# Top-32 attention and expert layer: the mask and the exponential of a score row by two ScalarE passes

## The chip, the core and the metric

The kernel runs on one core of a Trainium2 chip. The time is the device time of one execution in microseconds, as a median over runs. TensorE (PE in the profile) multiplies matrices, VectorE (DVE) and ScalarE (ACT) work on rows of 128 partitions, GpSimd (POOL) takes simple passes over data outside PSUM, and SyncE (SP) issues the DMAs.

## What is computed

Two layers follow each other. The first is attention over 4 batches of 8 heads, 576 positions and 64 channels, in which each row of scores keeps only its 32 largest entries. The second is a layer of 8 experts, to which every token goes, weighted by a gate matrix P that is normalised by rows and columns eight times.

```python
scores = scale * np.matmul(q, k.transpose(0, 1, 3, 2))
kth = np.partition(scores, -top_k, axis=-1)[..., -top_k:-top_k + 1]
scores = np.where(scores >= kth, scores, -1000000000.0)
scores = scores - np.max(scores, axis=-1, keepdims=True)
attn = np.exp(scores)
attn = attn / (np.sum(attn, axis=-1, keepdims=True) + 1e-09)
attn_out = np.matmul(attn, v)
...
for e in range(E):
    h = np.maximum(x @ w1[e], 0.0)
    out += P[:, e:e + 1] * (h @ w2[e])
```

## The kernel before

**Attention.** A unit is a tile of 128 score rows by 576 columns. There are 144 of them: 64 pairs of two heads (`attend_phase`), and 16 single ones for the left-over rows (`rest_weights`). For each unit TensorE writes the scores into the one PSUM buffer `sp` (L118, L119), and ScalarE copies them into one of three buffers `s` (`copy_scores`, L125 and L127). `topk` then finds the 32nd largest entry on VectorE: four rounds of an instruction that gives the eight largest (L138), with the ones already found overwritten in a work tile `w` between the rounds (L145). After the first round GpSimd makes the negative maximum `nb` (L140), and ScalarE the exponential of the whole row into `Et` (L141). After the fourth round VectorE compares the scores with the 32nd and multiplies the exponential with the result (L147), which also gives the row sum into `st`. `normalise` adds a small number on GpSimd (L151), inverts on VectorE (L152) and scales on ScalarE (L154). TensorE transposes the weights (L235), they are split into a high and a low part, `ath` and `atl`, multiplied with the values, and summed into `xt` (L252).

**Experts.** The seven entries of `STAGES` say which blocks of 256 tokens attention makes in which order; the first three stages have 8 pairs of units each. The gate matmuls of a stage (L337) come at its end. When a block is ready it boards a seat (`board`) and is taken past the eight experts in turns (`visit`: L420 and L507, evictions at L469, L470 and L515). Weights are split on ScalarE and GpSimd (L77, L83). While the first stage still runs, `first_half` makes partial products of the first block at low priority (L450). The last four blocks go through `hidden_pair` and `last_outputs` (L618, L677), after all of attention, after the gate's normalisation and after `right_factors`.

**Order.** A scheduler puts the instructions of each engine in a fixed order when the program is built. Attention has high priority, evictions of expert products a higher one, and expert matmuls fill the rest. On the chip each engine runs its list in order, and waits at its head.

Of the kernel before, what the change touches and what calls it, by code (L numbers as in the profile page):

```python
# [7 lines left out]
F32 = mybir.dt.float32  # L8
F32R = mybir.dt.float32r
AF = mybir.ActivationFunctionType  # L10
OP = mybir.AluOpType
# [7 lines left out]
NFT = F // 128  # L19
TOPK = 32  # L20
LOWEST = -3.0e38

# [21 lines left out]
def kernel(  # L46
# [11 lines left out]
    nc = tc.nc  # L58
# [14 lines left out]
    ap_ = actx.enter_context(tc.tile_pool(name="ap", bufs=2, side="right"))  # L73
# [56 lines left out]
    def topk(units):  # L130
        n = len(units)
        ws = [ap_.tile([128, S], F32, name="w", bufs=2) for _ in units]
        m8 = [ap_.tile([128, 4, 8], F32, name="m8", bufs=6) for _ in units]
        nb = [ap_.tile([128, 1], F32, name="nb", bufs=6) for _ in units]
        for r in range(4):
            for u in range(n):
                s, Em, rsum = units[u]
                nc.vector.max(m8[u][:, r, :], ws[u] if r else s)  # L138
                if r == 0:
                    nc.gpsimd.tensor_scalar(nb[u], m8[u][:, 0, 0:1], -0.125, 1.0, op0=OP.mult, op1=OP.mult)  # L140
                    nc.scalar.activation(Em, s, AF.Exp, bias=nb[u], scale=0.125)  # L141
            for u in range(n):
                s, Em, rsum = units[u]
                if r < 3:
                    nc.vector.match_replace(ws[u], m8[u][:, r, :], ws[u] if r else s, LOWEST)  # L145
                else:
                    nc.vector.scalar_tensor_tensor(Em, s, m8[u][:, 3, 7:8], Em,  # L147
                                                   op0=OP.is_ge, op1=OP.mult, accum_out=rsum)

    def normalise(Et, st, n):  # L150
        nc.gpsimd.tensor_scalar(st[:, 0, 0:n], st[:, 0, 0:n], 1e-9, 1.0, op0=OP.add, op1=OP.mult)  # L151
# [61 lines left out]
    def attend_phase(hp, qs, qm, ks, xt, xm, off):  # L213
# [3 lines left out]
        for t in range(2):  # L217
            Et = ap_.tile([128, 2, S], F32, name="Et", bufs=2)
            st = ap_.tile([128, 2, 2], F32, name="st", bufs=3)
            units = []  # L220
            for i in range(2):
                o = i * 256 + t * 128
                qc = qs[:, o:o + 128]
                sp = scores([((a, 0, 288), [(qc, ks[i], slice(a * 288, a * 288 + 288))]) for a in range(2)])
                units.append((copy_scores(sp[:, :, 0:288]), Et[:, i, :], st[:, 0, i:i + 1]))
            topk(units)
            normalise(Et, st, 2)
            cs = slice(t * 128, (t + 1) * 128)
            Ef = Et.rearrange("p a b -> p (a b)")
            for g in range(3):  # L230
                ps = pst.tile([128, 4, 128], F32, name="pt")
                for r in range(3):
                    j = g * 3 + r
                    o = j * 128 if j < 4 else (j * 128 + 128 if j < 8 else 512)
                    nc.tensor.transpose(ps[:, r, :], Ef[:, o:o + 128], idt)  # L235
                put = evac_pool if g < off else evac
                put(ath[:, g * 3:g * 3 + 3, cs], atl[:, g * 3:g * 3 + 3, cs], ps[:, 0:3, :])
# [20 lines left out]
    def rest_weights(qm, ks, put):  # L258
        Et = ap_.tile([128, 2, S], F32, name="Et", bufs=2)
        st = ap_.tile([128, 2, 2], F32, name="st", bufs=3)  # L260
        qa, qb = qm[:, 0:128], qm[:, 128:256]
        sp = scores([
            ((0, 0, 256), [(qa, ks[0], slice(0, 256)), (qb, ks[1], slice(64, 320))]),
            ((0, 256, 512), [(qa, ks[0], slice(256, 512)), (qb, ks[1], slice(320, 576))]),
            ((1, 0, 64), [(qa, ks[0], slice(512, 576)), (qb, ks[1], slice(0, 64))]),
        ])
        topk([(copy_scores(sp.rearrange("p a b -> p (a b)")[:, 0:S]), Et[:, 0, :], st[:, 0, 0:1])])
        normalise(Et, st, 1)
        ps = pst.tile([128, 4, 128], F32, name="pt")
        for j in range(4):  # L270
            nc.tensor.transpose(ps[:, j, :], Et[:, 0, j * 128:(j + 1) * 128], idt)
        for i in range(2):
            put(slice(0, 128), slice(4 * i, 4 * i + 4), ps[:, :, i * 64:(i + 1) * 64])
        ps = pst.tile([128, 4, 128], F32, name="pt")
        nc.tensor.transpose(ps[0:64, 0, :], Et[:, 0, 512:576], idt)
        nc.tensor.transpose(ps[:, 1, :], Et[:, 0, 448:576], idt)
        for i, r in enumerate((va, vb)):
            put(r, 8, ps[r, i, r])
# [504 lines left out]
```

## Time and profile before

| What | Value |
|---|---|
| Median of 3 runs | 1977.47 us |
| Lowest and highest run | 1975.19 and 1978.46 us |
| Profiled execution: span from first to last instruction (the page gives no other time of it) | 1976.5 us |
| Mean granted TensorE clock, as a share of full speed | 0.979 |
| ScalarE busy | 1042.2 us (53%) |
| GpSimd busy | 1094.3 us (55%) |
| DMA traffic | 240.02 MB, 121 GB/s of HBM over the span |

Busy time of an engine is the time in which it had an instruction in work; the rest of the span it waited, at the head of its list, for another engine, a buffer or a DMA. Matmuls overlap, and their ends are modelled, so that TensorE's busy time shows where it had work and not how close to its peak it ran. Busy time of different engines overlaps and does not add up to the span.

### The profile page before, as it was taken

Reading aid. Unit: us, or ns where it says so; the run is one execution under the profiler, and the core shown is the slowest. Engines: PE = TensorE matmul, PEld = TensorE weight load, DVE = VectorE, ACT = ScalarE, POOL = GpSimd, SP = SyncE. Lnnn points to the kernel's source line nnn. Section 1 sums busy time; section 2 is a strip of 40 time slices with the busy share of each in tenths; the row PEclk is TensorE's granted clock in tenths of the full one; section 3 lists DMA queues with packets and bytes.
Section 4 is the critical chain, followed back from the end, with each engine's and each line's share of the span. In section 5 each row is a group of like instructions: output and inputs, shape, how many; then the busy total and the mean of one; then the engine's idle time right before and its main releaser. Section 6 shows DMA issues by size and latency. Waiting matters only on the chain.

```text
span 1976.5 us, 27330 instructions
## 1 busy us (share of the span) xinstructions
PE 1886.2 (95%) x9617; PEld 1591.8 (81%) x9617; DVE 1468.7 (74%) x2828; ACT 1042.2 (53%) x1705; POOL 1094.3 (55%) x978
## 2 busy tenths in 40 slices
PE   4798899899999999999999999999999999999998
PEld 3687788898888888888788888888888888888887
DVE  8999999999999999948999982225555555543333
ACT  5777767665666666655665654453333333333331
POOL 4558867546655544545544548984454544545440
PEclk8899999999999999999999998999999999999999
DMA  3477654434433423443423333543333333311111
GB/s 115 129 243 258 206 183 156 147 105 132 132 109 122 132 83 98 153 143 123 129 84 120 99 107 107 182 155 110 102 102 112 112 112 101 102 59 54 59 38 43
DMA packets 96073, 240.02 MB, mean 121 GB/s; under 512 B 10816, under 2 KB 12992, under 8 KB 95936
## 3 DMA queue, kind: packets, MB, share of 16 engines
q1 hardware_dynamic: 95936, 238.28, 37.6%
q8 instruction: 75, 1.23, 0.3%
q14 instruction: 62, 0.51, 0.1%
HBM read 203.64 MB, written 34.60 MB: 121 GB/s over the span
## 4 chain that ended last, share of the span: by engine, by line
PE 53%; DVE 36%; POOL 3%; DMA 3%; issue 3%; ACT 2%; SPq 0%; POOLq 0%; ACTq 0%; DVEq 0%
PE p L677 18%; DVE m L138 12%; DVE w L145 10%; PE p L618 9%; PE p L420 7%; PE p L507 7%; DVE Et L147 6%; PE pc L618 5%; DVE hl L470 3%; DVE atl L86 3%; PE pb L618 2%; POOL wl L83 2%; DMA wr<-in_w_dram 1%; PE p L450 1%; PE pt L235 1%
## 5 line engine op out<-in xcount | busy, mean ns | idle before, releaser
L83 POOL TENSOR_TENSOR wl<-wr,wh 128x1024 fp32r<-128x1024 f32 x280 | 681.4, 2445 | 423.8 <-ACT wh L77 408.0
L77 ACT ACTIVATE wh<-wr 128x1024 fp32r<-128x1024 f32 x280 | 294.5, 1059 | 276.8 <-PE p L618 183.5
L138 DVE MAX8 m<-w 128x8 f32<-128x576 f32 x432 | 317.0, 747 | 1.4
L420 PE MATMUL p<-xh,wh 128*128 128x256 f32 (+1 forms) x768 | 267.3, 348 | 9.2 <-DVE hl L470 9.2
L420 PE MATMUL p<-xh,wl 128*128 128x256 f32 (+1 forms) x768 | 263.9, 344 | 0.0
L420 PE MATMUL p<-xl,wh 128*128 128x256 f32 (+1 forms) x768 | 263.5, 343 | 0.0
L507 PE MATMUL p<-wh,hh 128*128 128x512 f32 x640 | 253.8, 400 | 7.0 <-ACT hh L469 7.0
L507 PE MATMUL p<-wl,hh 128*128 128x512 f32 x640 | 252.9, 398 | 0.0
L507 PE MATMUL p<-wh,hl 128*128 128x512 f32 x640 | 245.6, 396 | 1.9 <-DVE hl L470 1.9
L524 DVE SCALAR_TENSOR_TENSOR acc<-p,P,acc 128x512 f32<-128x512 f32 x120 | 89.5, 750 | 166.6 <-PE p L677 166.6
L145 DVE MATCH_REPLACE8 w<-m,w 128x576 f32<-128x576 f32 x288 | 212.8, 740 | 0.2
L677 PE MATMUL p<-wh,h2h 128*128 128x512 f32 x512 | 199.8, 391 | 1.3 <-ACT h2h L641 0.7
L677 PE MATMUL p<-wl,h2h 128*128 128x512 f32 x512 | 199.9, 390 | 0.0
L677 PE MATMUL p<-wh,h2l 128*128 128x512 f32 x512 | 196.7, 390 | 0.0
L147 DVE SCALAR_TENSOR_TENSOR Et<-s,m,Et 128x576 f32<-128x576 f32 x144 | 172.5, 1203 | 2.5 <-ACT Et L141 2.0
L420 PEld LDWEIGHTS p<-xh,wh 128*128 128x128 f32 x768 | 148.8, 194 | 29.9 <-DVE hl L470 13.9
L470 DVE SCALAR_TENSOR_TENSOR hl<-p,hh 128x512 fp32r<-128x512 f32 x160 | 108.1, 678 | 79.9 <-ACT hh L469 79.2
L420 PEld LDWEIGHTS p<-xl,wh 128*128 128x128 f32 x768 | 148.8, 194 | 15.0 <-DVE xl L86 0.3
L420 PEld LDWEIGHTS p<-xh,wl 128*128 128x128 f32 x768 | 148.7, 194 | 14.3
L507 PEld LDWEIGHTS p<-wh,hh 128*128 128x128 f32 x640 | 121.3, 190 | 29.3 <-ACT hh L469 8.4
L507 PEld LDWEIGHTS p<-wh,hl 128*128 128x128 f32 x640 | 120.7, 189 | 25.0 <-DVE hl L470 2.7
L507 PEld LDWEIGHTS p<-wl,hh 128*128 128x128 f32 x640 | 121.6, 190 | 22.7
(174 smaller groups left out, 4039.1 us busy)
## 6 DMA issues: line engine op xcount, KB each, us to landing
wr<-in_w_dram SPq DMA_DIRECT2D x240, 512.0 KB, 3.5
y<-y SPq DMA_DIRECT2D x160, 256.0 KB, 2.7
raw<-in_k_dram SPq DMA_DIRECT2D x56, 288.0 KB, 3.1
wr<-in_w_dram SPq DMA_DIRECT2D x48, 256.0 KB, 3.8
raw<-in_q_dram SPq DMA_DIRECT2D x32, 256.0 KB, 2.8
p<-y SPq DMA_DIRECT2D x32, 256.0 KB, 3.5
y<-p SPq DMA_DIRECT2D x32, 256.0 KB, 4.5
raw<-in_v_dram SPq DMA_DIRECT2D x28, 288.0 KB, 3.0
```

Of the source, the lines that this page charges most:

```text
L77: nc.scalar.activation(dst, src, AF.Copy)
L83: nc.gpsimd.tensor_tensor(dst, src, hi.bitcast(F32), op=OP.subtract)
L86: nc.vector.tensor_tensor(dst, src, hi.bitcast(F32), op=OP.subtract)
L138: nc.vector.max(m8[u][:, r, :], ws[u] if r else s)
L145: nc.vector.match_replace(ws[u], m8[u][:, r, :], ws[u] if r else s, LOWEST)
L147: nc.vector.scalar_tensor_tensor(Em, s, m8[u][:, 3, 7:8], Em, op0=OP.is_ge, op1=OP.mult, accum_out=rsum)
L420: nc.tensor.matmul(ps[:, fo, :], a[:, kk, fs], x[:, k0 + kk, cs], start=(i == 0), stop=(i == 3 * nk - 1))
L470: nc.vector.scalar_tensor_tensor(seat.hl[:, ft, cs], src, 0.0, seat.hh[:, ft, cs].bitcast(F32), op0=OP.max, op1=OP.subtract)
L507: nc.tensor.matmul(ps, a[:, ft, ts], m[:, ft % 2, :], start=(i == 0), stop=(i == 3 * NFT - 1))
L524: return nc.vector.scalar_tensor_tensor(ACC[t], y, g, ACC[t], op0=OP.mult, op1=OP.add)
L618: nc.tensor.matmul(ps, w[:, kk, :], x[:, kk, :], start=(fresh and i == 0), stop=(i == 5), skip_group_check=True)
L677: nc.tensor.matmul(ps, a[:, ft, ts], m[:, ft, :], start=(i == 0), stop=(i == 11))
```

## The change

The exponential no longer runs early. VectorE's compare-and-multiply goes. When the 32nd largest entry t of a row is known, ScalarE makes two passes over the unit. The first is a Prelu of t - s: entries at or above t give zero or a negative number that is multiplied by a slope of 2 to the power -100, entries below t stay positive and large. The second is an exponential that undoes the slope in its scale, so that kept entries give exp(0.125 (s - max)) and the others nothing, and it leaves the row sum. Its bias `eb` is a new small VectorE instruction for each pair (0.125 t + nb), and `nb` is now made once for a pair. Maxima, `nb` and `eb` now have one tile each for a pair.

```diff
--- before.py
+++ after.py
@@ -19,6 +19,10 @@
 NFT = F // 128
 TOPK = 32
 LOWEST = -3.0e38
+
+
+
+KEPT = 2.0 ** -100
 
 
 
@@ -130,22 +134,22 @@
     def topk(units):
         n = len(units)
         ws = [ap_.tile([128, S], F32, name="w", bufs=2) for _ in units]
-        m8 = [ap_.tile([128, 4, 8], F32, name="m8", bufs=6) for _ in units]
-        nb = [ap_.tile([128, 1], F32, name="nb", bufs=6) for _ in units]
+        m8 = ap_.tile([128, 2, 4, 8], F32, name="m8", bufs=3)
+        nb = ap_.tile([128, 2], F32, name="nb", bufs=3)
+        eb = ap_.tile([128, 2], F32, name="eb", bufs=3)
         for r in range(4):
             for u in range(n):
-                s, Em, rsum = units[u]
-                nc.vector.max(m8[u][:, r, :], ws[u] if r else s)
-                if r == 0:
-                    nc.gpsimd.tensor_scalar(nb[u], m8[u][:, 0, 0:1], -0.125, 1.0, op0=OP.mult, op1=OP.mult)
-                    nc.scalar.activation(Em, s, AF.Exp, bias=nb[u], scale=0.125)
-            for u in range(n):
-                s, Em, rsum = units[u]
-                if r < 3:
-                    nc.vector.match_replace(ws[u], m8[u][:, r, :], ws[u] if r else s, LOWEST)
-                else:
-                    nc.vector.scalar_tensor_tensor(Em, s, m8[u][:, 3, 7:8], Em,
-                                                   op0=OP.is_ge, op1=OP.mult, accum_out=rsum)
+                nc.vector.max(m8[:, u, r, :], ws[u] if r else units[u][0])
+            if r == 0:
+                nc.gpsimd.tensor_scalar(nb[:, 0:n], m8[:, 0:n, 0, 0], -0.125, 1.0, op0=OP.mult, op1=OP.mult)
+            if r < 3:
+                for u in range(n):
+                    nc.vector.match_replace(ws[u], m8[:, u, r, :], ws[u] if r else units[u][0], LOWEST)
+        nc.vector.scalar_tensor_tensor(eb[:, 0:n], m8[:, 0:n, 3, 7], 0.125, nb[:, 0:n],
+                                       op0=OP.mult, op1=OP.add)
+        for u, (s, Em, rsum) in enumerate(units):
+            nc.scalar.activation(Em, s, AF.Prelu, bias=m8[:, u, 3, 7:8], scale=-1.0, alpha=KEPT)
+            nc.scalar.activation(Em, Em, AF.Exp, bias=eb[:, u:u + 1], scale=-0.125 / KEPT, accum_out=rsum)
 
     def normalise(Et, st, n):
         nc.gpsimd.tensor_scalar(st[:, 0, 0:n], st[:, 0, 0:n], 1e-9, 1.0, op0=OP.add, op1=OP.mult)
```

Lines after `KEPT` stand four further down in the new file up to the change, so that L81 in it is L77 before, L131 is L127, L155 to L158 are L151 to L154; L142 and L147 are the old L138 and L145, and L148, L151 and L152 are new. The scheduler orders the whole program anew. The places that matter are on VectorE and ScalarE.

VectorE, first stage, before: the end of the first pair (maxima `m8_150` and `m8_151`, weights `Et_132`) and the beginning of the second (`m8_220`, `m8_221`).

```order
L138 MAX m8_150<-w_148 128x8
L138 MAX m8_151<-w_149 128x8
L147 SCALAR_TENSOR_TENSOR Et_132,st_133<-s_139,m8_150,Et_132 128x576
L145 MATCH_REPLACE w_218<-m8_220,s_209 128x576
L145 MATCH_REPLACE w_149<-m8_151,w_149 128x576
L138 MAX m8_220<-w_218 128x8
L138 MAX m8_221<-s_216 128x8
L138 MAX m8_151<-w_149 128x8
L145 MATCH_REPLACE w_218<-m8_220,w_218 128x576
L147 SCALAR_TENSOR_TENSOR Et_132,st_133<-s_146,m8_151,Et_132 128x576
L145 MATCH_REPLACE w_219<-m8_221,s_216 128x576
L138 MAX m8_220<-w_218 128x8
```

The same place in the changed program, where `m8_150` belongs to the first pair and `m8_219` to the second.

```order
L142 MAX m8_150<-w_148 128x8
L142 MAX m8_150<-w_149 128x8
L147 MATCH_REPLACE w_217<-m8_219,s_208 128x576
L147 MATCH_REPLACE w_149<-m8_150,w_149 128x576
L142 MAX m8_219<-w_217 128x8
L142 MAX m8_219<-s_215 128x8
L142 MAX m8_150<-w_149 128x8
L147 MATCH_REPLACE w_217<-m8_219,w_217 128x576
L148 SCALAR_TENSOR_TENSOR eb_152<-m8_150,nb_151 128x2
L147 MATCH_REPLACE w_218<-m8_219,s_215 128x576
L142 MAX m8_219<-w_217 128x8
L142 MAX m8_219<-w_218 128x8
```

The two masks are gone from between the maxima; one `eb` stands two instructions behind the pair's last maximum, and maxima of the second pair stand on both sides of it.

ScalarE, before, from the fourth score copy on: `s_216` is the second unit of the second pair, `s_335` the first of the third.

```order
L127 ACTIVATE s_216<-sp_211 128x576
L141 ACTIVATE Et_202<-s_216,nb_223 128x576
L127 ACTIVATE s_335<-sp_330 128x576
L154 ACTIVATE Et_132<-Et_132,st_133 128x576 x2
L162 ACTIVATE tl_182<-pt_178 128x384
L77 ACTIVATE ath_130<-tl_182 128x3x128
L141 ACTIVATE Et_328<-s_335,nb_348 128x576
L162 ACTIVATE tl_190<-pt_186 128x384
L77 ACTIVATE ath_130<-tl_190 128x3x128
L127 ACTIVATE s_342<-sp_337 128x576
```

And in the changed program, where `s_215` is the fourth copy and `s_333` the fifth.

```order
L151 ACTIVATE Et_132<-s_139,m8_150 128x576
L131 ACTIVATE s_215<-sp_210 128x576
L151 ACTIVATE Et_132<-s_146,m8_150 128x576
L152 ACTIVATE Et_132,st_133<-Et_132,eb_152 128x576 x2
L131 ACTIVATE s_333<-sp_328 128x576
L158 ACTIVATE Et_132<-Et_132,st_133 128x576 x2
L166 ACTIVATE tl_181<-pt_177 128x384
L151 ACTIVATE Et_201<-s_208,m8_219 128x576
L81 ACTIVATE ath_130<-tl_181 128x3x128
L131 ACTIVATE s_340<-sp_335 128x576
L166 ACTIVATE tl_189<-pt_185 128x384
```

Before, the exponentials stand behind the score copies of their own units and ahead of the mask. Now the Prelus and exponentials of the first pair (L151, L152) stand ahead of the fifth copy, with the fourth copy between the two Prelus, and the scaling (L158) follows close behind. The table load stands once in each program, at the start:

```order
L77 ACT_TABLE_LOAD
```

```order
L81 ACT_TABLE_LOAD
```

## Rows read from the trace of the kernel before

**Rows 1.** Page, busy us (share of span) by engine, and tenths by slice

```profile
PE 1886.2 (95%) x9617; PEld 1591.8 (81%) x9617; DVE 1468.7 (74%) x2828; ACT 1042.2 (53%) x1705; POOL 1094.3 (55%) x978
...
PE   4798899899999999999999999999999999999998
...
DVE  8999999999999999948999982225555555543333
```

**Rows 2.** Stretches: length; busy us of PE, PEld, DVE, ACT, POOL; clock, DMA

```profile
0.00:138.00 138.00, 94.87 (x450) 78.21 (x450) 131.44 (x280) 93.20 (x167) 74.27 (x117) 0.88 0.50 156
138.00:274.00 136.00, 120.25 (x691) 103.61 (x689) 134.57 (x259) 96.39 (x157) 105.45 (x95) 0.94 0.67 220
274.00:407.00 133.00, 124.88 (x818) 113.23 (x819) 131.16 (x263) 85.66 (x142) 83.89 (x88) 0.97 0.48 156
407.00:575.00 168.00, 163.72 (x923) 142.25 (x922) 165.08 (x341) 109.84 (x187) 95.29 (x97) 0.99 0.40 126
575.00:1214.00 639.00, 632.45 (x3345) 536.64 (x3344) 565.91 (x1176) 396.25 (x686) 328.24 (x320) 0.99 0.36 115
1214.00:1310.00 96.00, 89.69 (x533) 79.97 (x533) 26.59 (x81) 42.30 (x54) 90.59 (x52) 0.96 0.48 154
1310.00:1976.00 666.00, 660.38 (x2868) 537.95 (x2866) 313.92 (x432) 218.58 (x316) 316.59 (x213) 1.00 0.28 88
```

**Rows 3.** Groups by line to 1214 us: busy us, mean ns, then idle before

```profile
L147 DVE SCALAR_TENSOR_TENSOR Et<-s,m,Et 128x576 f32<-128x576 f32 x144 | 172.5, 1203 | 2.5 <-ACT Et L141 2.0
...
L138 DVE MAX8 m<-s 128x8 f32<-128x576 f32 x144 | 107.2, 744 | 11.4 <-ACT s L127 7.7 <-ACT s L125 3.5
L141 ACT ACTIVATE Et<-s,nb 128x576 f32<-128x576 f32 x144 | 106.6, 774 | 15.6 <-POOL nb L140 8.9 <-PE pt L235 6.6
...
L235 PE MATMUL pt<-idt,Et 128*128 128x128 f32 x576 | 97.1, 288 | 12.0 <-ACT Et L154 5.8 <-DVE xt L252 3.2 <-DVE atl L86 2.6
...
L127 ACT ACTIVATE s<-sp 128x576 f32<-128x576 f32 x128 | 83.0, 649 | 89.3 <-DVE Et L147 78.1 <-PE sp L119 7.8 <-PE p L420 2.6
L118 PE MATMUL sp<-kh,qs 128*128 128x288 f32 x256 | 83.0, 335 | 42.4 <-ACT s L127 37.4 <-ACT kh L77 5.0
...
L140 POOL TENSOR_SCALAR nb<-m 128x1 f32<-128x1 f32 x144 | 33.2, 231 | 167.8 <-DVE m L138 138.0 <-DVE st L152 16.4 <-PE p L420 10.6
...
L152 DVE RECIPROCAL st<-st 128x2 f32<-128x2 f32 (+1 forms) x80 | 11.9, 149 | 3.6 <-POOL st L151 3.5
...
L147 DVE DVE_READ_ACCUMULATOR Et<-s,m,Et 128x1 f32 x144 | 11.2, 78 | 0.0
...
L340 ACT ACTIVATE lg<-pt 128x16 f32<-128x16 f32 (+1 forms) x10 | 1.7, 174 | 1.6 <-PE pt L337 1.6
...
L77 ACT ACT_TABLE_LOAD x1 | 1.3, 1283 | 0.7 <-PEq L773 0.7
```

**Rows 4.** Line L147: min/median/max ns; its busy us in four stretches

```profile
L147 DVE SCALAR_TENSOR_TENSOR Et<-s,m,Et x144: 792/814/2923, 17.8 to 1181.8; 128x576 f32<-128x576 f32 x144
...
0.00:138.00 138.00, 19.22 (x40) 0.88 0.50 156
138.00:274.00 136.00, 22.31 (x30) 0.94 0.67 220
274.00:407.00 133.00, 20.87 (x32) 0.97 0.48 156
407.00:575.00 168.00, 29.46 (x40) 0.99 0.40 126
```

**Rows 5.** Timeline: last mask, last xt and first gate matmuls of the first stage

```profile
109.78 0.81 DVE L147 SCALAR_TENSOR_TENSOR Et<-s,m,Et 128x576 f32<-128x576 f32 x1
...
136.11 0.88 DVE L252 TENSOR_TENSOR xt<-pt,tmp 64x256 f32<-64x256 f32 x2
...
137.94 0.73 PE L337 MATMUL pt<-wgs,xt 128*128 128x8 f32 x6
```

**Rows 6.** Waits, 0 to 138 us: us in total, times, longest

```profile
PE sp L118 <- ACT s L127: 27.9, 11, 4.8
```

## Prediction

> **What bounds the kernel now.** I read the page's busy shares and slices first, then the same by stretches. On the page TensorE is busy for 1886.2 of 1976.5 us and VectorE for 1468.7, most of the latter in the first 24 of 40 slices [rows 1]. So two things must be told apart: what VectorE limits, and what TensorE limits. The stretches do that [rows 2]; I cut them where the attention stages end. TensorE's idle time (length of the stretch minus its busy time) is 43.1 us in the first stage (0 to 138), 15.8 in the second (138 to 274), 8.1 in the third, 4.3 in the fourth, 6.6 in the 639 us after that, 6.3 in the hand-over at 1214, and 6.1 in the last 666 us. VectorE, on the other hand, is busy for 131.4 of 138, 134.6 of 136, 131.2 of 133 and 165.1 of 168 us in the first four stages. The reader is to see that up to about 575 us VectorE has no gap worth the name while TensorE has some 71 us of them, and that from 575 us on TensorE is full, whatever VectorE does. A shorter VectorE program can therefore pay early, and hardly later: faster attention later merely leaves more expert matmuls for afterwards. All idle time together is 90.3 us, so 1886 us is a floor under any such change.
>
> Who is late in the first stage is seen in the waits: TensorE's score matmuls L118 waited 27.9 us for the score copy on ScalarE [rows 6], and that copy, L127, sat 78.1 us in all (to 1214 us) until the mask L147 on VectorE had given an s buffer back [rows 3]. So the chain is mask, s buffer, copy, sp bank, next scores.
>
> **The change part by part.**
>
> *Removed from VectorE.* 144 masks L147 of 1203 ns mean and 144 accumulator reads of 78 ns: 172.5 + 11.2 = 183.7 us [rows 3]. One mask takes 792 ns at best and 2923 at worst [rows 4]. By stages the two together are 19.2 us for 20 masks in the first (0.96 each), 22.3 for 15 (1.49 each), 20.9 for 16 (1.30) and 29.5 for 20 (1.47) [rows 4], where the counts hold mask and read.
>
> *Added to VectorE.* 80 small instructions for eb, one a pair of tiles (16 of them for one tile). Nothing like it runs now. The reciprocal of the same shape takes 149 ns [rows 3]: the lower bound. But eb is the operation of L147, with two tiles read from the same memory, and L147's mean stands 0.41 us over its own best; with that excess eb takes 0.56 us, the upper bound. I take the upper one, because the row it rests on is the same operation. That is 45 us over the kernel (12 by the lower bound). The Trainium skill (GPSIMD Engine Reference, section Specifications) says that GpSimd shares its SBUF interfaces with VectorE and contends with VectorE instructions that have two SBUF inputs. The spread of L147 from 792 to 2923 ns agrees with it; by that rule eb inherits the wait, and without it the sum for eb would be the 12 us.
>
> *Added to ScalarE.* The exponential stays, and a Prelu of the same shape with the same kind of bias is added: 0.774 us, as L141 [rows 3]. The exponential now also leaves a row sum. What this costs on ScalarE no row shows: below it is nothing, above it the smallest instruction that ScalarE runs, 0.174 us (L340), and VectorE's own accumulator read is 0.078. I take 0.08. So each tile adds 0.85 us, bounds 0.77 and 0.95: 122 us over the kernel (111 to 137), on an engine that is busy for 93.2 of 138, 96.4 of 136, 85.7 of 133 and 109.8 of 168 us in the first four stages [rows 2]. With 20 more tiles in the first stage it would be 110, with 16 in the second 110: about nine tenths of stages that have become shorter. It is not a bound, but little room is left. The Trainium skill (ScalarE: Activation LUTs, Rules for kernel authors) would have maxima and multiplications on VectorE and not on ScalarE, for bf16 speed; no run here shows bf16, and by the rows in fp32 the mask with its read is 1.28 us there against 0.85 here. A switch of activation tables, 1283 ns each [rows 3], is excluded: the order shows one load at the start of both programs.
>
> *GpSimd.* One nb for a pair instead of two: 144 x 0.231 becomes 80 x 0.231, -15 us. It was mostly waiting there (167.8 us idle before L140 [rows 3]), so I count nothing for it.
>
> *Latency.* The mask came straight after the fourth maximum, 1.28 us. Now the last tile's Prelu and two exponentials follow each other, 0.77 + 2 x 0.85 = 2.5 us, so each stage ends 1.2 us later than VectorE's saving alone would say. The s buffer is freed by the Prelu, and the score copy of the next tile stands behind it on ScalarE: that is the new wait. VectorE has work on another tile meanwhile, as the order shows (m8_219 between rows of m8_150).
>
> **The sum.** First stage: its sixteenth mask starts at 109.8 us and the last xt at 136.1 [rows 5], so 16 masks lie ahead of its end: -16 x 0.96 + 8 x 0.56 + 1.2 = -9.7 us (with the lower eb -13.0; nothing if ScalarE eats it in the 26 us of scaling, transposing and splitting that follow the last mask). TensorE has not enough work there to object. Second stage: VectorE alone would give -16 x 1.49 + 8 x 0.56 = -19.3; TensorE can give at most its 15.8 us of idle, and GpSimd at 105.5 and ScalarE at 110 us of work stand near 120. I take half of VectorE's, -9.7; bounds 0 and -15.8. Its granted clock of 0.94 [rows 2] I leave as it is: the low level (1.2 GHz) shows in that mean, and fewer gaps may give some back. Third and fourth stage: idle 12.4 us, half of it, -6; bounds 0 and -12.4. From 575 to 1214 us I count nothing; bound -6.6. What would cost there if TensorE's cover were gone is not to be feared, since the expert matmuls cover the attention chain. At the hand-over GpSimd is busy for 90.6 of 96 us and not touched: 0, bounds -6 and +6. Sum -25.4, so 1951 against the profiled span of 1976.5. The page gives no other time of that execution; its span lies 1.0 under the median of the runs, 1977.47. So I predict 1952. All lower bounds together give -53.8, that is 1923 to 1924.
>
> **The rivals.**
>
> *Larger gain.* VectorE's whole saving comes through until TensorE is full: the -53.8 just worked out, 1924. For it: VectorE is the gapless one in every early stage. Against: ScalarE and GpSimd both come near the length of the stage. Chance 0.13.
>
> *No change.* ScalarE takes up what VectorE gives: the 26 us at the end of a stage run largely over ScalarE (for a pair two scalings and three evictions, then two copies), and if queueing behind the added passes lengthens it by the 9 us saved, the stages end when they did: 1973 to 1981, 1977 as its value. For it: about nine tenths busy. Against: of its 44.8 idle us in the first stage much was waiting for others. Chance 0.14.
>
> *Slower.* A wait takes the place of the mask: ScalarE runs in order, and a Prelu or an exponential at its head that waits for VectorE's fourth maximum or for eb holds up the score copy and the expert evictions behind it. Now TensorE waits 37.4 us for score copies [rows 3]. If that and its 5.8 us for scaled Et [rows 3] double, 43 us are added against 25 gained: 1995. It decides once VectorE's own wait for scores (11.4 us before L138, 0.16 for each of 72 pairs [rows 3]) passes the saving per pair of about 2 us. Chance 0.18.
>
> *Forecast.* 1935 to 1968 with 1952 in it: 0.55.
>
> **How the numbers follow.** 0.2%, about what a measurement of this kernel can tell from no change, is 4 us: 1973.5 to 1981.4 is the same. Faster are the forecast, the larger gain and half of the no-change case where it ends just short: 0.55 + 0.13 + 0.07 = 0.75. Same is the other half of that case, 0.07, and slower the 0.18. The range goes from 1922 (the larger gain) to 1980, past the no-change case; outside it lie most of the slower case and a rest of the larger gain, 0.2.
>
> **What would show it.** VectorE busy 1297 to 1330 us instead of 1468.7, ScalarE 1153 to 1179 instead of 1042.2. The first gate matmuls at about 128 us instead of 137.9 [rows 5]; TensorE's idle time to 575 us near 46 instead of 71, and after 575 us unchanged. eb between 0.15 and 0.56 us. I am wrong if the first gate does not move (ScalarE has the tail), if TensorE's waits for score copies grow, or if the time goes far below 1924, which would mean that TensorE was not full after 575 us.

## The result, and the profile after

The changed kernel takes 1946.97 us in the median of four runs (1944.40 to 1950.14), beside 1976.33 us for the kernel before in the same comparison (1973.37 to 1978.46). The ratio is 0.9847, with an interval from 0.9831 to 0.9864: 29.4 us, or 1.5%, faster. The profiled execution has a span of 1945.2 us and a mean granted clock of 0.989 (before 0.979).

From the page of the changed kernel: the busy times, the slices of TensorE and VectorE, and the shares of the chain that ended last.

```profile
PE 1874.1 (96%) x9617; PEld 1590.8 (82%) x9617; DVE 1351.9 (70%) x2620; ACT 1145.8 (59%) x1993; POOL 1057.5 (54%) x914
...
PE   4799889999999999999999999999999999999998
...
DVE  8979999999988998469998823135555555543333
...
PE 82%; DVE 12%; DMA 2%; ACT 1%; issue 1%; POOL 1%; SPq 0%; ACTq 0%; POOLq 0%; DVEq 0%
```

The same shares before:

```profile
PE 53%; DVE 36%; POOL 3%; DMA 3%; issue 3%; ACT 2%; SPq 0%; POOLq 0%; ACTq 0%; DVEq 0%
```

Beside [rows 1], VectorE has lost 117 us and ScalarE has gained 104. In the chain TensorE's share went from 53% to 82% and VectorE's from 36% to 12%: the chain that ended last now runs over TensorE for most of the way. TensorE runs the same 9617 matmuls.

The stretches of the changed kernel, cut where its own stages end (length; busy us of PE, PEld, DVE, ACT, POOL; clock, DMA):

```profile
0.00:137.00 137.00, 98.47 (x459) 82.41 (x459) 123.47 (x264) 107.88 (x210) 68.83 (x107) 0.96 0.50 161
137.00:262.00 125.00, 110.77 (x653) 97.94 (x653) 114.21 (x228) 103.11 (x182) 94.83 (x86) 0.93 0.70 227
262.00:383.00 121.00, 115.20 (x748) 104.41 (x749) 117.32 (x246) 95.16 (x174) 73.22 (x80) 0.97 0.46 147
383.00:533.00 150.00, 146.44 (x898) 131.75 (x897) 146.54 (x312) 117.23 (x219) 86.66 (x92) 0.99 0.44 140
533.00:1155.00 622.00, 620.12 (x3274) 527.02 (x3273) 507.57 (x1056) 446.67 (x823) 309.18 (x283) 0.99 0.36 116
1155.00:1276.00 121.00, 120.06 (x719) 107.11 (x719) 30.29 (x87) 56.38 (x71) 108.08 (x58) 1.00 0.51 166
1276.00:1945.00 669.00, 663.08 (x2880) 540.13 (x2878) 312.50 (x432) 219.32 (x317) 316.66 (x214) 1.00 0.28 88
```

Beside [rows 2], TensorE's idle time by stage is 38.5, 14.2, 5.8, 3.6, 1.9, 0.9 and 6.1 us, where it was 43.1, 15.8, 8.1, 4.3, 6.6, 6.3 and 6.1. That is 71.1 instead of 90.3 us: 19.2 of the 31.3 us by which the span is shorter. The other 12.1 us are busy time of the same matmuls, beside a higher mean granted clock; most of that rise stands in the first stretch (0.88 to 0.96) and at the hand-over (0.96 to 1.00).

VectorE now has 13.5 us of gaps in the first stage (6.6 before), and ScalarE is busy for 107.9 of 137 us (93.2 of 138 before). The groups of lines up to 1214 us show who waits:

```profile
L142 DVE MAX8 m<-s 128x8 f32<-128x576 f32 x144 | 107.9, 749 | 50.6 <-ACT s L131 25.8 <-ACT s L129 24.1
...
L122 PE MATMUL sp<-kh,qs 128*128 128x288 f32 x256 | 84.1, 340 | 30.0 <-ACT s L131 19.6 <-POOL qs L87 5.3 <-ACT kh L81 4.9
L131 ACT ACTIVATE s<-sp 128x576 f32<-128x576 f32 x128 | 82.9, 648 | 14.2 <-PE sp L123 13.5
L148 DVE SCALAR_TENSOR_TENSOR eb<-m,nb 128x2 f32<-128x2 f32 (+1 forms) x80 | 44.1, 552 | 0.7
```

In [rows 3] the score copy sat idle for 89.3 us, 78.1 of them for the mask; now it is 14.2, nearly all of it for the scores themselves. TensorE's wait for score copies fell from 37.4 to 19.6 us. Turned round, VectorE's first maximum waited 50.6 us where it had waited 11.4: VectorE is now partly the one that waits for ScalarE.

Two starting times divide the gain. The first gate matmul of the changed kernel (minimum, median, maximum ns; first and last start in us):

```profile
L341 PE MATMUL pt<-wgs,xt x128: 170/256/299, 136.8 to 1148.7; 128*128 128x8 f32 x128
```

It starts 1.1 us earlier than in [rows 5]. The first matmul of the last four blocks (`hidden_pair`), in the kernel before and then in the changed one:

```profile
L618 PE MATMUL p<-B11h,wh x64: 387/395/398, 1306.9 to 1919.6; 128*128 128x512 f32 x64
```

```profile
L622 PE MATMUL p<-B11h,wh x64: 392/395/398, 1275.7 to 1888.3; 128*128 128x512 f32 x64
```

It starts 31.2 us earlier, and from there to the end both take the same (669.5 us). So nearly everything was won between the end of the first stage and the hand-over, and almost nothing in the first stage, which I had given 9.7 us.

### The profile page after: what moved, and what is told of

The parts are those of the page before. It is cut to its first block, busy times and chain, and to the rows that moved or that the text cites. A ratio compares the mean times of both kernels' runs of the same rounds, so it can differ in the third digit from the quotient of the medians.

```text
span 1945.2 us, 27297 instructions
## 1 busy us (share of the span) xinstructions
PE 1874.1 (96%) x9617; PEld 1590.8 (82%) x9617; DVE 1351.9 (70%) x2620; ACT 1145.8 (59%) x1993; POOL 1057.5 (54%) x914
## 4 chain that ended last, share of the span: by engine, by line
PE 82%; DVE 12%; DMA 2%; ACT 1%; issue 1%; POOL 1%; SPq 0%; ACTq 0%; POOLq 0%; DVEq 0%
PE p L511 18%; PE p L681 18%; PE p L424 18%; PE p L622 9%; DVE m L142 5%; PE pc L622 5%; DVE w L147 4%; PE pb L622 2%; PE pt L239 2%; PE p L454 2%; PE sp L123 2%; PE sp L122 2%; PE pt L252 2%; PE pt L253 2%; DVE hl L474 1%
## 5 line engine op out<-in xcount | busy, mean ns | idle before, releaser
L81 ACT ACTIVATE wh<-wr 128x1024 fp32r<-128x1024 f32 x280 | 296.2, 1060 | 297.8 <-PE p L622 194.4
L142 DVE MAX8 m<-w 128x8 f32<-128x576 f32 x432 | 318.6, 749 | 2.9
L424 PE MATMUL p<-xl,wh 128*128 128x256 f32 (+1 forms) x768 | 261.4, 341 | 1.7 <-DVE xl L90 1.7
L147 DVE MATCH_REPLACE8 w<-m,w 128x576 f32<-128x576 f32 x288 | 213.3, 741 | 0.1
L142 DVE MAX8 m<-s 128x8 f32<-128x576 f32 x144 | 107.9, 749 | 50.6 <-ACT s L131 25.8
```

What stands on the lines that cost most here:

```text
L81: nc.scalar.activation(dst, src, AF.Copy)
L142: nc.vector.max(m8[:, u, r, :], ws[u] if r else units[u][0])
L147: nc.vector.match_replace(ws[u], m8[:, u, r, :], ws[u] if r else units[u][0], LOWEST)
L424: nc.tensor.matmul(ps[:, fo, :], a[:, kk, fs], x[:, k0 + kk, cs], start=(i == 0), stop=(i == 3 * nk - 1))
```

## The experiments

Twelve kernels, each compared with the kernel before. Of e1 and e2, which leave work out, only the times are of use. "Gate" is the start of the first gate matmul, "pair" that of the first matmul of `hidden_pair`, in the profiled execution.

| Run | Median us | Ratio to before, 95% | Gate | Pair |
|---|---|---|---|---|
| before (profiled) | 1975.37 to 1976.38 | 1 | 137.9 | 1306.9 |
| the change | 1946.97 | 0.9831 to 0.9864 | 136.8 | 1275.7 |
| e1_half_first_new | 1949.09 | 0.9853 to 0.9882 | 154.8 | 1277.8 |
| e2_half_first_old | 1967.90 | 0.9955 to 0.9976 | 144.0 | 1293.0 |
| e3_vector_split_new | 1953.73 | 0.9878 to 0.9908 | 131.4 | 1281.4 |
| e4_vector_split_old | 1992.17 | 1.0073 to 1.0105 | 140.8 | 1318.5 |
| e5_new_in_first_three | 1967.66 | 0.9942 to 0.9975 | 138.3 | 1298.5 |
| e6_new_after_three | 1965.46 | 0.9932 to 0.9962 | 141.0 | 1294.4 |
| e7_grouping_alone | 1983.31 | 1.0021 to 1.0048 | 138.8 | 1313.6 |
| e8_vector_time_back | 2006.74 | 1.0140 to 1.0179 | 142.0 | 1332.4 |
| e9_factors_on_vector_old | 1968.75 | 0.9948 to 0.9980 | 138.4 | 1300.6 |
| e10_no_shift_new | 1943.24 | 0.9816 to 0.9846 | 135.9 | 1271.8 |
| e11_no_shift_factors_new | 1947.83 | 0.9839 to 0.9869 | 138.7 | 1278.0 |
| e12_second_prelu_new | 1967.36 | 0.9926 to 0.9967 | 150.6 | 1298.7 |

**Is it VectorE's time that pays?** Two runs. The first adds a compare-and-multiply on VectorE to the changed kernel, of the old mask's form, on the work tile that nobody reads afterwards.

```diff
+        for u in range(n):
+            nc.vector.scalar_tensor_tensor(ws[u], ws[u], m8[:, u, 3, 7:8], ws[u],
+                                           op0=OP.is_ge, op1=OP.mult)
```

> The changed kernel with a compare-and-multiply of the old size per tile back on VectorE (on the work tile, its result not used), so that VectorE has its 144 passes of about 1.2 us again while ScalarE keeps the new ones and frees the score buffers. If VectorE's time is what the gain came from: 1970 to 1990 us, and above 1976 if ScalarE's added passes then cost something of their own. If the gain came from the score buffers being freed by ScalarE: 1945 to 1960 us.

The groups of lines to 1250 us have the added instruction:

```profile
L149 DVE SCALAR_TENSOR_TENSOR w<-w,m 128x576 f32<-128x576 f32 x144 | 175.9, 1222 | 0.6
```

It costs what the mask did (1203 ns in [rows 3]), VectorE's busy time rises by 153 us to 1504.8, and the kernel by 59.8 us to 2006.74, past the kernel before and past the 1990 that was expected at most. The ScalarE passes are the same in both. The added instruction stands ahead of `eb`, so it also lengthens the way to the exponential, as the old mask did. That early freed score buffers are what pays is excluded: ScalarE frees them here as in the change, and the score copy hardly waits, which in [rows 3] it did for 89.3 us.

```profile
L131 ACT ACTIVATE s<-sp 128x576 f32<-128x576 f32 x128 | 82.5, 644 | 3.1 <-PE sp L123 2.2
```

So what the change won, it won by taking this work off VectorE.

The second leaves VectorE's mask and ScalarE's early exponential where they were and takes over only the common tiles of a pair for maxima and `nb`.

> Maxima and nb grouped by pairs as in the changed kernel, but the exponential early and the mask on VectorE as before. Both theories: 1971 to 1981 us, no gain from the grouping (64 fewer nb of 0.23 us on a GpSimd that mostly waited there). A rival, that fewer GpSimd instructions and semaphores are what helped: 1950 to 1965 us.

It takes 1983.31 us, 7.9 more than the kernel before beside it (1975.40) and above the 1971 to 1981 expected, though GpSimd has 64 instructions fewer. So the move of the mask is worth 36.3 us (1983.31 to 1946.97), and the grouping that came with it takes about 7 of them back. Why the grouping costs was not followed further. Set beside e8 it says a second thing: with the work back on VectorE and the added passes on ScalarE, the kernel is 23.4 us slower than with the mask alone (2006.74 and 1983.31). That is about what the new passes and `eb` cost where VectorE isn't relieved.

**Where is it won?** The same kernel with the new passes in the first 24 pairs only (the first three stages), and with them everywhere else, the mask in the rest; tiles grouped in both. `late` says that a pair takes the new passes; in the second kernel its condition is turned round.

```diff
+        made.append(1)
+        late = len(made) <= 24
...
+                if not late:
+                    for u, (s, Em, rsum) in enumerate(units):
+                        nc.scalar.activation(Em, s, AF.Exp, bias=nb[:, u:u + 1], scale=0.125)
...
+                elif not late:
+                    nc.vector.scalar_tensor_tensor(Em, s, m8[:, u, 3, 7:8], Em,
+                                                   op0=OP.is_ge, op1=OP.mult, accum_out=rsum)
...
+        if not late:
+            return
```

> The new passes in the first three stages only (24 pairs), the masks on VectorE after that; maxima and nb grouped by pairs throughout. The forecast's theory (the gain is made before 575 us) expects nearly all of it here: 1946 to 1955 us. What the trace of the changed kernel suggests instead (3 us in the first stage, 8 to 10 more by 430 us, the rest after 930 us, most of it at the hand-over) expects about a third: 1961 to 1969 us, with the first expert pair matmul near 1296 us.

> The reverse: masks on VectorE in the first three stages, the new passes from the fourth on. The forecast's theory: 1965 to 1974 us. The trace's reading: two thirds of the gain, 1953 to 1962 us, since attention ends some 35 us earlier among the expert work and the hand-over is covered.

The first, 1967.66, falls into the second of its two ranges; the second, 1965.46, lies at the edge of the first theory's range and above the other's. Both ranges were counted from the kernel before, without the price of the grouping. Measured against the grouped kernel with the mask, the early third is worth 15.6 us and the rest 17.9: together 33.5 of 36.3. The gain is not an early one that the rest merely keeps. About half comes from pairs behind the third stage, to which the sum had given no more than half of the fourth stage's 4.3 us of idle time, and nothing after 575 us.

**What holds the first stage?** Four runs bear on it. The first leaves half of the partial products of `first_half` out, so that TensorE has less to do there.

```diff
-                        for kk in range(2):
+                        for kk in range(1):
```

> The changed kernel with half of the early partial products (L454) left out, so its output lacks that part. In the changed kernel the first gate matmuls start at 136.8 us, 1 us earlier than before, though VectorE reached the eighth pair's last maximum some 14 us earlier. Theory L (TensorE runs its list in order, and the slow L454 matmuls that stand in it ahead of the gate set the time): about 18 us of them go from ahead of the gate, so the first gate falls to 122 to 128 us, and the whole kernel to 1925 to 1937 us. Theory C (the splitting of the weights over ScalarE's tl copy and GpSimd, with one tl buffer, sets the time): the first gate stays at 134 to 138 us and the kernel at 1935 to 1947 us, since only expert work becomes less.

> The kernel before with the same half of the partial products left out. If VectorE with its masks held the first stage of the kernel before, the first gate stays at 133 to 138 us here, and e1 gains more against the changed kernel than e2 does against the kernel before. If TensorE's list held both (theory L in its strong form), the gate falls here as well, to 122 to 130 us. Theory C: stays at 134 to 138 us. The kernel at 1955 to 1975 us.

Neither theory foresaw this: the gate came later, at 154.8 and 144.0 us, and the changed kernel took 1949.09 us, more than either range. With fewer partial products the scheduler placed the first expert matmul of the changed kernel at 129.0 instead of 157.5 us, and the weight splits for it on ScalarE and GpSimd with it. Nothing speaks for theory L: with fewer matmuls ahead of it the gate wasn't earlier, and TensorE was idle for 60.7 of 155 us. Since the edit moved other work too, the two runs say no more than that.

The next two undo an exception of the first stage. There the 24 groups of transposed weights are copied by ScalarE into the one tile `tl`, rounded from it to `ath` on ScalarE, and subtracted on GpSimd for `atl`. Without the exception VectorE subtracts straight from PSUM, and the copy falls away.

```diff
-OFF = {(0, 0): 3}
+OFF = {}
```

> The changed kernel with the first stage's weights split on VectorE, straight from PSUM, as in the other stages: no tl copy on ScalarE (24 of 0.49 us) and no split on GpSimd (24 of 1.0 us) there, 24 splits of 0.54 us more on VectorE. Theory C: the chain per group loses one ScalarE pass and one buffer, the first gate falls to 122 to 130 us and the kernel to 1933 to 1941 us. Theory L: gate at 133 to 137 us, since the same L454 matmuls stand ahead of it; the kernel at 1942 to 1950 us.

> The kernel before with the first stage's weights split on VectorE. If VectorE holds its first stage, 24 splits of 0.54 us push the first gate out to 143 to 151 us and the kernel to 1980 to 1990 us. If theory C held already there, the gate falls to 128 to 135 us and the kernel to 1968 to 1975 us.

In the changed kernel the gate comes 5.4 us earlier, at 131.4: between the two ranges. In the kernel before it comes 2.9 us later, at 140.8, again between the ranges, although 24 splits more, 13 us, stand on a VectorE that was busy for 131.4 of 138 us [rows 2]. Both kernels took longer than any range had it, 1953.73 and 1992.17 us. Over the whole the changed kernel loses 7 us by it: its next stages end at 254.5, 385.7 and 539.4 us (261.4, 382.3 and 532.7 in the change), so that the lead is gone in the third stage.

The fourth issues each Prelu twice and gives ScalarE 111 us more.

```diff
             nc.scalar.activation(Em, s, AF.Prelu, bias=m8[:, u, 3, 7:8], scale=-1.0, alpha=KEPT)
+            nc.scalar.activation(Em, s, AF.Prelu, bias=m8[:, u, 3, 7:8], scale=-1.0, alpha=KEPT)
```

> The changed kernel with each Prelu made twice: 144 x 0.77 = 111 us more on ScalarE and nothing else. If ScalarE is near its limit in the early stages, as the forecast had it (it is busy for 108 of 137, 103 of 125 and 95 of 121 us there): 1958 to 1978 us. If it has room: 1945 to 1953 us.

Its first gate matmul:

```profile
L342 PE MATMUL pt<-wgs,xt x128: 170/256/363, 150.6 to 1200.2; 128*128 128x8 f32 x128
```

The 20 more Prelus of that stage are 15.5 us of ScalarE's time, and the gate came 13.8 us later: nearly one for one. (The mean granted clock of its first 151 us is 0.90 beside 0.96; TensorE is idle for 43.7 us of them.) Over the kernel the 111 us cost 20.4, within the first range. So in the first stage of the changed kernel there is no room left on ScalarE's way. The second Prelu lies both in ScalarE's queue and on the way of its own unit; the run doesn't tell the two apart.

**Why does the hand-over give something?** Here GpSimd makes most of the factors that `hidden_pair` needs (`right_factors`). I gave VectorE this work, in the kernel before:

```diff
-                lo_pool(l[:, :, cs], src, h[:, :, cs])
+                lo_dve(l[:, :, cs], src, h[:, :, cs])
...
-            nc.gpsimd.tensor_tensor(dst, a, b, op=OP.subtract)
+            nc.vector.tensor_tensor(dst, a, b, op=OP.subtract)
```

> The kernel before with the differences and low parts of the right factors, some 25 us of GpSimd work at the hand-over, made on VectorE instead, which is busy for 27 of 96 us there. Theory H (about 10 us of the change's gain come at the hand-over, where GpSimd was 94% busy, because attention now ends further ahead of the expert work that covers it): relieving GpSimd directly gives the kernel before the same, 1964 to 1971 us, with the first expert pair matmul near 1297 instead of 1307 us. If the hand-over was not GpSimd's: 1973 to 1981 us.

```profile
L618 PE MATMUL p<-B11h,wh x64: 392/395/398, 1300.6 to 1913.2; 128*128 128x512 f32 x64
```

It takes 7.6 us less, as expected, and `hidden_pair` begins 6.3 us earlier, although TensorE is no further than before when attention ends (some 2 us behind, by the estimate described in the next section). So relieving GpSimd of the factors does relieve the hand-over. How, is shown in part only. The stretch between attention and `hidden_pair` of this run (columns as in [rows 2]), and TensorE's waits in the same stretch of the kernel before (1214 to 1310 us: in total, times, longest):

```profile
1208.00:1301.00 93.00, 88.86 (x561) 79.82 (x561) 44.42 (x105) 46.84 (x63) 80.61 (x36) 1.00 0.48 160
```

```profile
PE pt L393 <- DVE cs L391: 3.4, 2, 2.4
PE p L507 <- ACT hh L469: 2.2, 1, 2.2
PE p L420 <- DVE hl L470: 0.7, 1, 0.7
```

TensorE is idle for 4.1 us instead of 6.3, and its granted clock is 1.00 instead of 0.96. Its own waits before were for the gate's normalisation (L393) and for evictions, none of them for GpSimd; through which instructions the factors held it stays open.

The same in the changed kernel, together with the next edit:

> The same with the right factors on VectorE as in e9. Theory H: TensorE is idle for only 0.9 us at the hand-over of the changed kernel, so nothing is left to win, within 4 us of e10. If GpSimd's load still holds something: 5 to 10 us below e10.

There it wins nothing: 1947.83 beside 1943.24 without it, 4.6 us more. With the change (here without the shift by the maximum), the hand-over no longer gains by relieving GpSimd.

**Is VectorE still worth relieving?** `nb` and `eb` are left out, and the exponential goes without a bias.

```diff
-            nc.scalar.activation(Em, Em, AF.Exp, bias=eb[:, u:u + 1], scale=-0.125 / KEPT, accum_out=rsum)
+            nc.scalar.activation(Em, Em, AF.Exp, scale=-0.125 / KEPT, accum_out=rsum)
```

> The changed kernel without the shift by the maximum: the exponential is taken of 0.125 (s - t), t the 32nd largest, so nb and eb go altogether (80 eb of 0.55 us on VectorE, 80 nb on GpSimd) and the exponential waits for the Prelu alone. A row's weights are the same after the division by their sum, but for the 1e-9 added to it. If VectorE's time still sets part of the time: the change took 117 us from VectorE and 31 from the span, so another 44 gives about 12, 1931 to 1940 us. If TensorE is full and the rest is start and ScalarE: 1943 to 1949 us.

VectorE is busy for 31.5 us less (1320.4), the kernel takes 3.7 us less, and the two intervals overlap. ScalarE is relieved a little too: without a bias tile the exponential takes 685 ns in the mean instead of 775, and ScalarE is busy for 11 us less. Its time is the lowest of all that ran. The gate stays at 135.9 us. Where 113 us of VectorE's time brought 36 (the grouped kernel to the change), the next 31 bring hardly anything: VectorE's time sets little of the rest.

## Why the prediction was right, and where its sum was not

The direction and the size of the whole held: 1952 predicted, 1946.97 measured, 29.4 us gained where the sum had 25.4. But the terms lie elsewhere, and that the total came so near is in part luck: by the estimate below, the first four stages gave about 12 of the 25.4 us, and some 19 came where the sum had nothing.

**First stage: -9.7 predicted, -1.1 measured. This step failed.** Its first half was right: VectorE is about as much earlier as the lower `eb` would have it, as its rows in the timeline of the changed kernel show (start, length, what; idle before and releaser in brackets):

```profile
96.21 0.13 DVE L148 SCALAR_TENSOR_TENSOR eb<-m,nb 128x2 f32<-128x2 f32 x1
...
106.28 0.88 DVE L256 TENSOR_TENSOR xt<-pt,tmp 64x256 f32<-64x256 f32 x2
...
117.35 0.76 DVE L142 MAX8 m<-s 128x8 f32<-128x576 f32 x1 [7.55 <-ACT s L131]
...
134.51 0.42 DVE L256 TENSOR_TENSOR xt<-pt,tmp 64x256 f32<-64x256 f32 x1
135.69 0.43 DVE L256 TENSOR_TENSOR xt<-pt,tmp 64x256 f32<-64x256 f32 x1
```

The stage's eighth `eb` is done at 96.3 us, where the sixteenth mask began at 109.8 [rows 5]. But the last `xt` is done at 136.1 instead of 137.0. ScalarE's rows of the same stretch have the tail, in the changed kernel:

```profile
100.28 1.44 ACT L158 ACTIVATE Et<-Et,st 128x576 f32<-128x576 f32 x2
...
108.47 0.49 ACT L166 ACTIVATE tl<-pt 128x384 f32<-128x384 f32 x1
108.99 0.52 ACT L81 ACTIVATE ath<-tl 128x384 fp32r<-128x384 f32 x1
...
112.79 0.48 ACT L166 ACTIVATE tl<-pt 128x384 f32<-128x384 f32 x1
...
114.21 1.43 ACT L151 ACTIVATE Et<-s,m 128x576 f32<-128x576 f32 x2
...
121.19 0.51 ACT L166 ACTIVATE tl<-pt 128x384 f32<-128x384 f32 x1
...
127.88 0.49 ACT L166 ACTIVATE tl<-pt 128x384 f32<-128x384 f32 x1
```

And in the kernel before, behind a row of VectorE:

```profile
105.53 0.88 DVE L252 TENSOR_TENSOR xt<-pt,tmp 64x256 f32<-64x256 f32 x2
...
107.81 0.48 ACT L162 ACTIVATE tl<-pt 128x384 f32<-128x384 f32 x1
...
110.62 0.65 ACT L127 ACTIVATE s<-sp 128x576 f32<-128x576 f32 x1 [1.77 <-DVE Et L147]
...
113.41 1.44 ACT L154 ACTIVATE Et<-Et,st 128x576 f32<-128x576 f32 x2 [0.37 <-DVE st L152]
...
119.38 0.65 ACT L127 ACTIVATE s<-sp 128x576 f32<-128x576 f32 x1 [0.87 <-DVE Et L147]
...
120.40 0.50 ACT L162 ACTIVATE tl<-pt 128x384 f32<-128x384 f32 x1
...
128.27 0.50 ACT L162 ACTIVATE tl<-pt 128x384 f32<-128x384 f32 x1
```

The eighth pair is scaled from 100.3 us on, 13.1 earlier than before (113.4). From there to the end of the last `xt` it was 23.6 us and is now 35.8: 12 us have gone into the tail. Six groups of transposed weights make up the last pair of heads. They go one after the other through the one `tl`, some 4 us apart, once the pair of heads ahead of them is through (its `xt` starts at 105.5 us before and at 106.3 now). The first group is copied at 107.8 and 108.5 us, the fourth, which is the eighth pair's first, at 120.4 and 121.2, the sixth at 128.3 and 127.9. So these groups run at nearly the same times in both kernels, and already in the kernel before the eighth pair's scaled weights waited 5.5 us for their turn; now they wait 19.5. The prediction had put the sixteenth mask on the path to the end of the stage, with 26 us behind it. The rows have the queue of groups there.

What ScalarE does between the groups is not the same. In the kernel before it stood idle there while it waited for masks and inverted row sums of VectorE (1.77, 0.37 and 0.87 us above). Now VectorE waits (7.55 us for a score copy), and ScalarE runs the Prelus, exponentials, scalings and copies of the next stage's units between the groups, whose maxima VectorE has finished early. The stretch from 111.8 to 132.5 us, before and then changed:

```profile
111.80:132.50 20.70, 19.09 (x99) 15.62 (x98) 20.70 (x46) 17.21 (x32) 11.28 (x16) 1.00 0.72 236
```

```profile
111.80:132.50 20.70, 19.45 (x106) 16.99 (x105) 15.08 (x35) 20.53 (x42) 9.48 (x13) 1.00 0.74 244
```

VectorE was busy throughout and is now busy for 15.1 us; ScalarE was busy for 17.2 of the 20.7 us and now for 20.5. This is the bound that the prediction named, "nothing if ScalarE eats it", and its reason for not taking it, that much of ScalarE's idle time was waiting, was too weak. That ScalarE's work counts there is also shown by the second Prelu (+13.8 us); that the path over `tl` is part of it, by its removal (-5.4 us); that it is not VectorE, by the run without `eb` (-0.9 us). How much of the tail is ScalarE's queue, and how much GpSimd and the one `tl` buffer, stays open: the removal takes both away.

**Second to fourth stage: -15.7 predicted, about -9 measured.** An estimate from the trace: I weighed each matmul with its usual duration and compared when both kernels had issued the same amount of work. (Between the gate and `hidden_pair` the lead moves by up to 5 us with the weights chosen; at these two points it hardly does.) The changed kernel leads by about 3 us at 150 us of the kernel before, by 10 at 413 and by 12 at 523. Half of VectorE's saving and half of the idle time were too much: of 28.2 us of idle time 4.6 went. The bounds held.

**575 to 1214: 0 predicted, about 7 by the estimate; bound 6.6.** By the same estimate the lead is 13 us from 626 to 938, and 20 at 1048. TensorE's idle time in this stretch fell from 6.6 to 1.9. TensorE was nearly full, but not quite. The run with the new passes behind the first three stages only speaks for the same: 18 us hang on what comes there, the hand-over included. Nor were TensorE's 1886 busy us the floor that the prediction took them for: the same matmuls are busy for 1874.1 us in the changed kernel, at a mean granted clock of 0.989 instead of 0.979. "Faster attention later merely leaves more expert matmuls for afterwards" was the wrong half of a right thought, as the next point shows.

**Hand-over: 0 predicted, 11 to 13 by the estimate; bounds 6 to either side. Here the step failed too, on the good side.** The last stage of attention ends at 1145.3 us instead of 1202.8, 57.5 earlier, while the lead in matmuls is about 20. So more expert matmuls were left for the time after attention. The prediction took them for a plain delay; but they fall where TensorE had been waiting, around the gate's normalisation and GpSimd's factors. The stretch between attention and `hidden_pair` grew from 96 to 121 us, and TensorE's idle time in it went from 6.3 [rows 2] to 0.9 us, its granted clock from 0.96 to 1.00. The lead grows from 18.6 us at 1202 (20 at 1048) to 31.2 at 1368. Of that the idle time accounts for 5.4 us, and the clock, as an estimate, for about 4 (0.04 of 96 us). The two runs with the factors on VectorE show it from the other side: 7.6 us to be had there before, none after.

**The prices.** The pair's `eb` takes 552 ns in the mean, where I took 560 because the mask's excess would be inherited. Its line, and that of the accumulator read on ScalarE (minimum, median, maximum):

```profile
L148 DVE SCALAR_TENSOR_TENSOR eb<-m,nb x80: 132/230/2396, 22.5 to 1111.5; 128x2 f32<-128x2 f32 x64, 128x1 f32<-128x1 f32 x16
...
L152 ACT ACTIVATION_READ_ACCUMULATOR Et<-Et,eb x144: 183/192/263, 23.4 to 1122.0; 128x1 f32 x144
```

The mean is that of short and long ones, as with the mask [rows 4], and the traces tell which are long. Of the 80 `eb`, 42 started while a GpSimd tensor-tensor instruction was in work, and took 914 ns in the mean; the other 38 took 151. Of the 144 masks before, 68 started so and took 1629 ns; the other 76 took 822. The Trainium skill (GPSIMD Engine Reference, section Specifications) says that GpSimd and VectorE contend for SBUF when VectorE reads two inputs from it; these rows agree with it, and no run here takes GpSimd away to show it. ScalarE's accumulator read takes 0.192 us, above my upper bound of 0.174 and more than twice the 0.08 that I took; over 144 tiles that is 16 us on ScalarE that I had not counted. The Prelu takes 0.772 to 0.776 us, as taken. ScalarE's busy time, 1145.8, still lies below the 1153 to 1179 expected, and VectorE's, 1351.9, above 1297 to 1330: with `eb` at its upper price 139 us should have gone, and 117 went. Both have one reason: the prediction added up durations, and neighbours in an engine's list overlap. All durations of VectorE together fell by 142 us, its busy time by 117; those of ScalarE rose by 141, its busy time by 104.

**The rival "slower"** named the right waits and the wrong weight. VectorE's wait for scores did rise, from 11.4 to 50.6 us, or 0.7 us for a pair, below the 2 us at which it would have decided; TensorE's wait for the copies fell. "No change" described the first stage exactly, and only that one. The Trainium skill (ScalarE: Activation LUTs, Rules for kernel authors) wants maxima and multiplications on VectorE, for its speed in bf16. This fp32 case doesn't bear that out: 1.28 us of VectorE became about 0.97 us of ScalarE, and the kernel 1.5% faster.

## What to carry to other kernels

Time taken from the engine that bounds pays until another engine's queue ends the stage: for each stage look whether the last instruction of the relieved engine is on the path to the end at all, or whether its result already waits in a queue behind it, before giving the stage its saving. Work that is released earlier does not only move: if the leftover falls on a later place where the main engine waits, as here at the hand-over, it is paid there. An edit that comes along, such as common tiles for a pair, has a price of its own and should be timed alone.

## What the runs showed of the hardware that I had not expected

A ScalarE pass with a row sum is followed by a separate accumulator read of 183 to 263 ns, more than twice VectorE's 78 ns [rows 3]. A VectorE instruction on 128x2 elements with two tiles took between 132 and 2396 ns: 914 in the mean where it started during a GpSimd tensor-tensor instruction, 151 where it didn't, so that its size says little about its price. A ScalarE exponential of 128x576 took 775 ns with a bias tile and 685 without one.
